# The start of a two-stage attention and feed-forward kernel: a row of maxima computed in two parts, one weight block converted two pairs later, and the second pair's maxima placed among the first pair's key tiles

## The chip, the cores and the metric

The kernel runs on one core of one Trainium2 chip. The metric is the device time of one execution in microseconds (us); a median of a few runs is given, and one further execution was profiled. Below, PE is the engine of matrix products, PEld its weight loads, DVE the vector engine, ACT the engine of activation functions, POOL the general engine, and SP the engine that only issues transfers here. Each runs its own instructions in order and waits for the others through semaphores.

## The reference

The first stage is an attention over 8 batches and 8 heads, with 1152 positions and a head size of 64. Queries are averaged over neighbouring positions, so that 576 remain. The second stage takes its 4608 rows of 512 numbers through a feed-forward block with the function h - tanh(h).

```python
q_pool = q.reshape(B, H, S // factor, factor, D).mean(axis=3)        # factor 2
scores = scale * np.matmul(q_pool, k.transpose(0, 1, 3, 2))
scores = scores - np.max(scores, axis=-1, keepdims=True)
attn = np.exp(scores)
attn = attn / (np.sum(attn, axis=-1, keepdims=True) + 1e-09)
attn_out = np.matmul(attn, v)
...
h = x @ w_in                                                         # 4608 x 512 by 512 x 2048
g = h - np.tanh(h)
return (g @ w_out).astype(np.float32)
```

## The kernel before

Two heads are worked on together as a *pair*: one lies in partitions 0 to 63, the other in 64 to 127. There are 32 pairs. The program numbers them from 0 (`pi`), so its `pi == 1` is "the second pair", or "pair 2", of the text.

For each pair the kernel does this:

- `load` (line 185) fetches the queries and keys, `load_v` (196) the values. `query_sums` (201) adds neighbouring queries: on DVE for the first pair, on POOL for the others.
- `hi_part` (209) makes a rounded copy of queries and keys on ACT, in three pieces; `lo_part` (213) makes what the rounding left out on DVE, in one piece of 1728 columns. Scores are products of these: hi by hi, hi by lo, lo by hi.
- `max_part` (217) computes a rough score tile for 128 queries by 384 keys, for both heads, from the hi parts alone, and DVE takes the largest of each row from PSUM. A pair needs fifteen: five tiles of queries (`t`) by three of keys (`c`).
- `max_rows` (229) takes the largest of the three key parts, negates it (tile `nm`), and turns it by a transpose (tile `tr`). Its inner `back` has SP write ten small transfers that lay the result out as one row per head (tile `mb`): for each `t` and each head one.
- `scores` (246) computes a tile of 128 keys by 288 queries (one half of the queries) for both heads: three products and a fourth, of ones with `mb`, which subtracts the maximum. ACT takes the exponential into a tile `p_f`.
- After the nine key tiles of a half, `pv` (269) multiplies the exponentials with the values. POOL adds the nine tiles up in three groups (`z_part`, 261), and after the second half PE sums those over the partitions (`z_sums`, 282).

Score tiles, rough score tiles, pv groups and two steps of a weight block all take their PSUM space from one pool of four buffers in turn (`banks`, 172). A tile can be written only when the one four places earlier has been read.

Beside this the attention stage converts the feed-forward weights, which arrive as 64-bit numbers, into a hi and a lo part. `w_block` (331) does one block of 128 by 512 weights over 75 units (below): it issues the load at unit `u`, has ACT and DVE begin at `u + 31` (one operation and three), DVE go on at `u + 49` (two), POOL add at `u + 50`, ACT split at `u + 66`, POOL subtract at `u + 68`, and SP store the result at `u + 75`. There are 32 blocks.

The order of all this is written out by hand. Time is cut into *units*: a pair has `U` = 36 of them, 18 to a half, and every second unit of a half has one score tile, with pv at the end of the half. `add(u, f, ...)` puts a step into a table for unit `u`; in each unit the tables run in the order `first`, `early`, the score tile, `at`, pv. The reduction of a rough score tile is put into `first` of the next unit. Units below 0 are what runs ahead of the first score tile. All engines keep this program order in the attention stage (`InOrder`, line 27), and SP's one queue of transfers too.

The steps of a pair are given as offsets from its first unit (lines 411 to 432). For the first pair the fifteen maxima stand at -60 to -46, the row at -43, its transfers at -42, the low part at -41, the values' load at -40. For the second pair, eight maxima stand at its offsets -54 to -38, which are units -18 to -2, and seven at units 0 to 16; its low part stands at unit 0, its row at 17, the transfers at 20. The third pair's loads stand at unit -14, its query sums at 1, its hi part at 17, and its first eight maxima at 18 to 34.

Weight blocks start at `36 * (i - 2) + 5`: block 1 at -31, block 2 at 5, block 3 at 41. Block 0 starts at 23.

The feed-forward stage then runs over chunks of 512 tokens, with sixteen slices of the hidden size in each; the change does not touch it.

In the profile nearly all operations of the attention stage carry line 37, that of the helper that records them. They are told apart by their tiles: `mx<-ps` is the reduction of a rough score tile, `p_f<-ps` the exponential, `ps<-p_f,v` pv, `mb<-tr` the row transfers, `w` and `w_raw` a weight block.

Of the kernel before, what the change touches and what calls it, by code (L numbers as in the profile page):

```python
# [12 lines left out]
ALU = mybir.AluOpType  # L13
AX = mybir.AxisListType
# [29 lines left out]
def kernel(  # L44
# [89 lines left out]
    t, n = chunks.pop()  # L134
# [4 lines left out]
    with ExitStack() as actx:  # L139

        sm = actx.enter_context(tc.tile_pool(name="sm", bufs=2))
        op = actx.enter_context(tc.tile_pool(name="op", bufs=1))
# [7 lines left out]
        pe, act, dve, pool, sp = (InOrder(tc, e) for e in (nc.tensor, nc.scalar, nc.vector, nc.gpsimd, nc.sync))  # L150
# [4 lines left out]
        U = 4 * KT  # L155
# [14 lines left out]
        at, first, early = {}, {}, {}  # L170
# [6 lines left out]
        def add(u, f, *args, at=at):  # L177
            at.setdefault(u, []).append(lambda: f(*args))
# [47 lines left out]
                pe.matmul(ps[:, h, 0:CH], w.hi[r, q0:q0 + P], w.hi[r, mv], start=True, stop=True)  # L226
            add(u + 1, lambda: dve.tensor_reduce(w.mx[:, :, t, c], ps[:, :, 0:CH], axis=AX.X, op=ALU.max), at=first)

        def max_rows(u, pi, step):

            w = pairs[pi]
            nm, tr = nms[w.i], sm.tile([P, 32], F32, name="tr")
            dve.tensor_reduce(nm[:, 0:10], w.mx.rearrange("p h t c -> p (h t) c"), axis=AX.X, op=ALU.max, negate=True)
            dve.transpose(tr, nm.bitcast(F32))

            def back():
                for t in range(5):
                    for h in range(2):
                        row, c = w.mb[64 * h:64 * h + 1].bitcast(F32), 5 * h + t
                        if t < 4:  # L240
                            sp.dma_start(row[:, t * P:(t + 1) * P].rearrange("p (g n) -> p g n", n=32), tr[c:P:32])
                        else:
                            sp.dma_start(row[:, t * P:].rearrange("p (g n) -> p g n", n=32), tr[P - (SQ - t * P) + c:P:32])
            add(u + step, back)
# [139 lines left out]
            for r in range(f // P, (f + WB) // P):  # L384
                blocks.append((1, r, 0))
        for i, blk in enumerate(blocks):
            u = U * (i - 2) + 5 if i else 23
            add(u, w_block, u, *blk)

        tot = []  # L390
# [20 lines left out]
        for pi in range(n_pair):  # L411
            u = pi * U
            units = dict(load=-86, query_sums=-71, hi=-55, lo=-36, load_v=-30)
            row, step = -19, 3

            spots = [x for half, us in ((-54, (2, 4, 8, 10, 12, 14, 16)), (-36, (2, 4, 8, 10, 14, 16)))
                     for x in [(early, half)] + [(at, half + i) for i in us]]
            if pi == 0:
                units.update(load=-70, query_sums=-62, hi=-60, lo=-41, load_v=-40)
                spots = [(at, -60 + i) for i in range(15)]  # L420
                row, step = -43, 1
            if pi == 1:
                units.update(load=-104, query_sums=-62)
            add(u + units["load"], load, pi)
            add(u + units["query_sums"], query_sums, pi, dve if pi < 1 else pool)
            for c in range(0, KQ, SQ):
                add(u + units["hi"], hi_part, pi, c, c + SQ)
            add(u + units["lo"], lo_part, pi)
            for i, (when, x) in enumerate(spots):
                add(u + x, max_part, u + x, pi, i // 3, i % 3, at=when)  # L430
            add(u + units["load_v"], load_v, pi)
            add(u + row, max_rows, u + row, pi, step)

        def run(u, at=at):

# [115 lines left out]
    for ci, (t0, n) in enumerate(chunks):  # L551
        x_h, x_l, _ = xs
        po = []
        for fc in range(NF):
# [3 lines left out]
            load = []  # L558
            if ci + 1 < len(chunks):
# [3 lines left out]
                load = [xs[2][(fc - x) // 3][i] for i, x in ((3, 3), (0, 0), (1, 2), (2, 2)) if (fc - x) % 3 == 0 and 0 <= fc - x < 3 * NP]  # L563
# [47 lines left out]
```

## Time and profile before

| what | value |
|---|---|
| median of 3 runs | 1610.8 us (1610.68 to 1611.51) |
| the profiled execution's own time | 1611.35 us |
| its span in the profile | 1609.6 us |
| PE busy | 1584.2 us, 98% |
| DVE busy | 1235.9 us, 77% |
| ACT busy | 1015.9 us, 63% |
| POOL busy | 1016.9 us, 63% |
| first pv group of the first pair starts | 44.49 us |
| second pv group of the first pair starts | 55.97 us |

A row of a timeline gives the start in us, the length in us, the engine, the line, the operation, the tile written and the tiles read, the shapes and how many instructions were merged; in brackets stands the idle time before it and what ended it. A row of a table of stretches gives start and end, the length, the busy time of PE, PEld, DVE, ACT and POOL with the number of instructions in brackets, the granted clock of PE as a share, the share of time in which the transfer engines were busy, and GB/s. Matmuls overlap: the step from one row's start to the next tells how fast they follow each other, the length of a row is longer.

### The profile page before, as it was taken

How to read it: one execution, taken by the hardware profiler on the slowest of the kernel's cores; microseconds unless marked ns; L12 is line 12 of the kernel's file. 1: busy time of each engine (PE TensorE's matmuls, PEld its weight loads, DVE VectorE, ACT ScalarE, POOL GpSimd, SP SyncE). 2: the span in 40 equal slices, each digit the busy share in tenths (PEclk: the TensorE clock that was granted, in tenths of full speed). 3: DMA queues.
4: the chain of work that ended last, by engine and by line, in shares of the span. 5: the costliest groups of instructions: out<-in, count | busy, mean ns of one | idle time of the engine just before them, and what ended most of it. 6: DMA issues, size and time to landing. Idle time of an engine off the chain costs nothing. (4 is left out here: it accounts for less than half of the span.)

```text
span 1609.6 us, 31923 instructions
## 1 busy us (share of the span) xinstructions
PE 1584.2 (98%) x12288; PEld 1233.6 (77%) x12288; DVE 1235.9 (77%) x1725; ACT 1015.9 (63%) x1833; POOL 1016.9 (63%) x760
## 2 busy tenths in 40 slices
PE   5999999999999999999999999999999999999999
PEld 3777777777777777777778888888888888888897
DVE  7888788787887888788567777767777777777786
ACT  1665665665665665666666666666665666666786
POOL 2899999999999999999845343334343343423332
PEclk9999999999999999999999999999999999999999
DMA  3343443443443443444474101111010111110100
GB/s 144 117 145 110 144 140 109 138 146 110 128 155 111 133 140 122 128 142 148 136 262 152 40 27 40 40 40 28 26 53 27 49 31 40 33 34 14 36 24 22
DMA packets 73433, 147.38 MB, mean 92 GB/s; under 512 B 12736, under 2 KB 37440, under 8 KB 73280
## 3 DMA queue, kind: packets, MB, share of 16 engines
q1 hardware_dynamic: 73280, 145.33, 27.4%
q8 instruction: 97, 1.59, 0.4%
q14 instruction: 56, 0.46, 0.1%
HBM read 109.20 MB, written 35.95 MB: 90 GB/s over the span
## 5 line engine op out<-in xcount | busy, mean ns | idle before, releaser
L37 DVE TENSOR_REDUCE mx<-ps 128x2 f32<-128x768 f32 x480 | 435.6, 953 | 111.3 <-PE ps L37 111.1
L37 POOL TENSOR_TENSOR g_lo<-g_s,g_hi 128x512 fp32r<-128x512 f32 (+1 forms) x160 | 190.8, 1192 | 482.7 <-ACT g_hi L514 445.0
L37 ACT ACTIVATE p_f<-ps 128x576 f32<-128x576 f32 x576 | 356.6, 651 | 78.9 <-PE ps L37 56.4
L37 PE MATMUL ps<-hi 64*128 64x288 f32 (+1 forms) x2112 | 316.3, 351 | 19.5 <-DVE mx L37 8.2
L37 PE MATMUL ps_h<-x,wi 128*128 128x512 f32 (+1 forms) x1440 | 318.3, 370 | 0.0
L37 PE MATMUL ps_o<-wo,g_hi 128*128 128x512 f32 x1008 | 311.5, 390 | 0.0
L37 POOL TENSOR_TENSOR z<-p_f 128x576 f32<-128x576 f32 x192 | 276.3, 1439 | 41.7 <-ACT p_f L37 39.9
L37 PE MATMUL ps<-p_f,v 128*64 128x288 f32 x2304 | 293.5, 409 | 0.0
L37 PEld LDWEIGHTS ps_h<-x,wi 128*128 128x128 f32 x1440 | 253.2, 188 | 50.4
L37 POOL TENSOR_TENSOR z<-z,p_f 128x576 f32<-128x576 f32 x192 | 273.3, 1423 | 15.0
L37 PEld LDWEIGHTS ps<-hi 64*128 64x128 f32 x2112 | 196.3, 187 | 91.0 <-issue 29.6
L37 PEld LDWEIGHTS ps<-p_f,v 128*64 128x64 f32 x2304 | 159.7, 137 | 113.9 <-ACT p_f L37 11.6
L503 ACT ACTIVATE g_u<-ps_h 128x512 f32<-128x512 f32 (+1 forms) x160 | 88.8, 555 | 235.7 <-PE ps_h L37 232.3
L508 DVE SCALAR_TENSOR_TENSOR ps_w<-g_u,ps_h 128x512 f32<-128x512 f32 (+1 forms) x160 | 103.0, 644 | 157.8 <-ACT g_t L504 157.2
L37 PEld LDWEIGHTS ps_o<-wo,g_hi 128*128 128x128 f32 x1008 | 187.6, 188 | 39.1
L37 PE MATMUL ps_o<-wo,g_lo 128*128 128x512 f32 x504 | 196.2, 389 | 0.0
L37 PE MATMUL ps<-hi,lo 64*128 64x288 f32 x1152 | 171.0, 293 | 0.0
L37 PE MATMUL ps<-lo,hi 64*128 64x288 f32 x1152 | 171.0, 293 | 0.0
L37 PE MATMUL ps<-mb,ones_k 64*128 64x288 f32 x1152 | 170.8, 293 | 0.0
L37 ACT ACTIVATE o_s<-ps 128x288 f32<-128x288 f32 x64 | 26.4, 412 | 218.5 <-PE ps L37 218.5
L513 DVE COPY_PREDICATED g_s<-g_m,g_t 128x512 f32<-128x512 int32 (+1 forms) x160 | 115.4, 721 | 16.8 <-DVE g_s L512 0.5
L511 DVE SCALAR_TENSOR_TENSOR ps_w<-g_s,ps_w 128x512 f32<-128x512 f32 (+1 forms) x160 | 102.9, 643 | 16.6 <-ACT g_m L507 0.5
(66 smaller groups left out, 2252.1 us busy)
## 6 DMA issues: line engine op xcount, KB each, us to landing
q_n<-in_q_dram SPq DMA_DIRECT2D x32, 576.0 KB
kq<-in_k_dram SPq DMA_DIRECT2D x32, 576.0 KB
v<-in_v_dram SPq DMA_DIRECT2D x32, 576.0 KB
x_dram<-o_s SPq DMA_DIRECT2D x32, 288.0 KB
out_dram<-o_s SPq DMA_DIRECT2D x34, 256.0 KB
w_raw<-in_moe_w_in_dram SPq DMA_DIRECT2D x16, 512.0 KB
wi_dram<-w_hl SPq DMA_DIRECT2D x16, 512.0 KB
w_raw<-in_moe_w_out_dram SPq DMA_DIRECT2D x16, 512.0 KB
```

Source lines behind the costliest of these rows:

```text
L37: ins = self.tc.keep_in_program_order(f(*args, **kwargs))
L503: nc.scalar.activation(u, h, AF.Square)
L508: nc.vector.scalar_tensor_tensor(w, u, -P0, h, op0=ALU.add, op1=ALU.mult)
L511: nc.vector.scalar_tensor_tensor(w, s2, P2, w, op0=ALU.add, op1=ALU.mult)
L513: last = nc.vector.copy_predicated(s1, m.bitcast(I32), th).ins
```

## The change

The first pair's row of maxima is made in two parts: `max_rows` takes a range of query tiles, and runs once for tiles 0 to 2 after nine maxima (unit -51) and once for tiles 3 and 4 after all fifteen (unit -43). Six transfers belong to the first part, four to the second. The load of the first pair's values moves from unit -40 to -50, just ahead of the first part's transfers.

Weight block 1 starts at unit 95 instead of -31; its first conversion then falls at unit 126, in the fourth pair.

For the second pair, the query sums move from unit -26 to -54 and the hi part from -19 to -46. All fifteen maxima stand at units 0 to 20 (twelve in the first half, three in the second), the low part at 18 instead of 0, the row at 21 and its transfers at 24. The first eight maxima of the third pair move from units 18 to 34 to units 22 to 34.

```diff
-        def max_rows(u, pi, step):
+        def max_rows(u, pi, step, t0=0, t1=5):
...
-            dve.tensor_reduce(nm[:, 0:10], w.mx.rearrange("p h t c -> p (h t) c"), axis=AX.X, op=ALU.max, negate=True)
+            dve.tensor_reduce(nm[:, 0:10].rearrange("p (h t) -> p h t", t=5)[:, :, t0:t1], w.mx[:, :, t0:t1], axis=AX.X,
+                              op=ALU.max, negate=True)
             dve.transpose(tr, nm.bitcast(F32))
 
             def back():
-                for t in range(5):
+                for t in range(t0, t1):
...
         for i, blk in enumerate(blocks):
-            u = U * (i - 2) + 5 if i else 23
+            u = U * (i - 2) + 5 if i > 1 else 23 + 2 * U * i
             add(u, w_block, u, *blk)
...
             if pi == 0:
-                units.update(load=-70, query_sums=-62, hi=-60, lo=-41, load_v=-40)
+                units.update(load=-70, query_sums=-62, hi=-60, lo=-42, load_v=-50)
                 spots = [(at, -60 + i) for i in range(15)]
                 row, step = -43, 1
+                add(u - 51, max_rows, u - 51, 0, 1, 0, 3)
             if pi == 1:
-                units.update(load=-104, query_sums=-62)
+                units.update(load=-104, query_sums=-90, hi=-82, lo=-18)
+                spots = [(early, -36)] + [(at, i - 36) for i in (1, 2, 4, 5, 7, 8, 10, 11, 13, 14, 16)] + [(early, -18), (at, -18), (at, -16)]
+                row = -15
+            if pi == 2:
+                spots[:8] = [(at, i - 72) for i in (22, 23, 25, 26, 28, 30, 32, 34)]
...
-            add(u + row, max_rows, u + row, pi, step)
+            add(u + row, max_rows, u + row, pi, step, 0 if pi else 3)
```

## The prediction

> **What bounds the kernel now.** I read the page's head, then stretches of ten microseconds (start and end, length, then busy time of PE, weight loads, DVE, ACT, POOL), then the waits of PE.
>
> ```profile
> span 1609.6 us, 31923 instructions
> PE 1584.2 (98%) x12288; PEld 1233.6 (77%) x12288; DVE 1235.9 (77%) x1725; ACT 1015.9 (63%) x1833; POOL 1016.9 (63%) x760
> ...
> 20.00:30.00 10.00, 5.51 (x20) 2.71 (x22) 9.80 (x12) 0.00 (x0) 0.00 (x0) 1.00 0.21 65
> 30.00:40.00 10.00, 5.17 (x38) 4.40 (x38) 6.56 (x7) 2.78 (x5) 5.83 (x3) 1.00 0.74 278
> ...
> PE ps L37 <- DVE mx L37: 8.2, 22, 2.6
> PE ps L37 <- ACT hi L37: 6.9, 1, 6.9
> PE ps L37 <- DVE w L37: 4.1, 1, 4.1
> PE ps L37 <- POOL z L37: 1.3, 1, 1.3
> ```
>
> PE is busy for 98% of the span, and its idle time of 25.4 us (1609.6 - 1584.2) lies almost wholly in the start: between 20 and 40 us PE is idle for 9.3 us. The waits name DVE's maxima and one wait of 4.1 us for a weight tile. A microsecond saved in the start should therefore come off the end, since from there on PE has next to nothing else to wait for. The timeline of the start shows why PE stops:
>
> ```profile
> 27.25 0.43 SPq L37 DMA_DIRECT2D w_raw<-in_moe_w_in_dram  x1
> 30.98 0.44 PE L37 MATMUL ps<-mb,ones_k 64*128 64x288 f32 x2
> 32.62 0.62 ACT L37 ACTIVATE ps<-w_raw 128x512 f32<-128x512 f32 x1 [21.69 <-DMA w_raw<-in_moe_w_in_dram]
> 33.18 1.17 ACT L37 ACTIVATE p_f<-ps 128x576 f32<-128x576 f32 x2
> 33.28 0.70 DVE L37 TENSOR_SCALAR ps<-ps 128x512 f32<-128x512 f32 x1 [3.33 <-ACT ps L37]
> 35.48 0.93 PE L37 MATMUL ps<-hi 64*128 64x384 f32 x4 [4.05 <-DVE w L37]
> ```
>
> PE has two score tiles ready at 31.4, but ACT, which runs in order, stands at the conversion of a weight block whose load was issued only at 27.25 and landed at 32.6. Both exponentials wait behind it; so does DVE, whose three operations on that block stand ahead of the next maxima. All four PSUM buffers are then held, and PE stops until 35.48. The load is late because SP, also in order, issues ten row transfers first:
>
> ```profile
> 7.58 13.06 DVE L37 TENSOR_REDUCE mx<-ps 128x2 f32<-128x768 f32 x15 [2.12 <-PE ps L37]
> 9.11 1.83 ACT L37 ACTIVATE hi<-kq 128x576 fp32r<-128x576 f32 x3 [1.73 <-POOL kq L37]
> 21.11 1.92 DVE L37 TENSOR_TENSOR lo<-kq,hi 128x1728 fp32r<-128x1728 f32 x1
> 21.28 5.49 SPq L37 DMA_DIRECT2D mb<-tr  x10
> 27.73 0.43 SPq L37 DMA_DIRECT2D q_n<-in_q_dram  x1
> ```
>
> DVE sets the pace of the start: fifteen maxima in 13.06 us (0.87 each), the row, the low part, and then eight maxima of the second pair ahead of the first score.
>
> **The change, part by part.** I count up to the start of the second probabilities-times-values group (pv) of the first pair, at 55.97. By there the changed order has put through the same maxima: fifteen of pair 1, fifteen of pair 2, eight of pair 3. I call a maximum "m" and a score tile "S"; these rows price them, with PE's slow cadence and its fast one:
>
> ```profile
> 38.23 0.61 PE L37 MATMUL ps<-hi 64*128 64x288 f32 x2 [0.78 <-DVE mx L37]
> ...
> 39.35 0.44 PE L37 MATMUL ps<-hi 64*128 64x288 f32 x2
> ...
> 40.31 0.76 PE L37 MATMUL ps<-hi 64*128 64x384 f32 x4
> 40.56 0.65 ACT L37 ACTIVATE p_f<-ps 128x576 f32<-128x576 f32 x1 [0.31 <-PE ps L37]
> 40.87 0.44 PE L37 MATMUL ps<-lo,hi 64*128 64x288 f32 x2
> ...
> 42.16 0.96 DVE L37 TENSOR_REDUCE mx<-ps 128x2 f32<-128x768 f32 x1 [0.32 <-PE ps L37]
> ...
> 43.11 0.30 PE L37 MATMUL ps<-lo,hi 64*128 64x288 f32 x2
> ...
> 44.49 4.59 PE L37 MATMUL ps<-p_f,v 128*64 128x288 f32 x36
> ...
> 49.82 0.29 PE L37 MATMUL ps<-hi 64*128 64x288 f32 x2
> 50.35 0.55 PE L37 MATMUL ps<-hi 64*128 64x384 f32 x4
> 50.74 0.30 PE L37 MATMUL ps<-lo,hi 64*128 64x288 f32 x2
> ...
> 52.85 4.42 DVE L37 TENSOR_REDUCE mx<-ps 128x2 f32<-128x768 f32 x5 [0.30 <-PE ps L37]
> ...
> 55.97 4.59 PE L37 MATMUL ps<-p_f,v 128*64 128x288 f32 x36
> ```
>
> Slow: S is 40.31 - 39.35 = 0.96, of four matmul pairs at 0.24; the next pairs (m, and the first of an S) take 0.56, so m is 0.32. Fast: S 0.53 (50.35 - 49.82), a matmul pair a quarter of it, 0.13, m 0.39 - 0.13 = 0.26. On DVE m is 0.88 back to back (4.42 / 5). A pv group is 4.5 at the fast cadence. The cadence rose at 43.1, 4.9 us after the last gap.
>
> *Row in two parts.* It adds a reduction, a transpose and no transfer (six and four for ten). From the end of the maxima at 20.64 to the low part at 21.11 the existing two cost 0.47 on DVE; this is paid once more, after nine maxima. The low part then runs 21.58 to 23.5. It is on the path: +0.47. The first six row transfers can go at about 16.0 (7.58 + 9 x 0.87 + 0.6) and at 0.55 each (5.49 / 10) are issued by 19.3, four microseconds before a score needs them; with one queue they were issued by 24.6. The other four go by 23.8 and are wanted only in the second half, after 38. The load of values now passes the rows on SP: one issue slot of some 0.4 us, long before 16.0.
>
> *Weight block moved.* ACT's 0.62 and DVE's five operations leave the first pair, and the wait for the load with them; nothing then stands ahead of the first exponential. SP reaches the third pair's loads near 24 rather than at 27.73.
>
> *Maxima of pair 2 behind the scores.* Query sums and high part move up in their queues without new work: ACT had run the high part by 10.9 us already, right after POOL's sums. DVE has no maxima between the low part and the first score. Now the first half, by hand: the first S can go on at 23.6. PE at 0.96 and 0.32 is continuous while slow, and DVE takes each m as it comes: the fourth leaves PE at 23.6 + 0.72 + 3 x 0.32 + 2 x 0.96 = 27.2 (the first was issued earlier) and is reduced by 28.35, with 0.2 from PE to the reader (ACT's row at 40.56 begins 0.25 after its tile's slot) and 0.96. After some 5 us the cadence rises, and DVE at 0.88 sets the pace through four buffers: the twelfth m can be issued when the tenth is reduced, at 28.35 + 6 x 0.88 = 33.6. Pv follows at about 34.05. Bounds: DVE without a gap, 23.5 + 10 x 0.88 + 0.5 = 32.8; PE slow throughout, 23.6 + 0.72 + 8 x 0.96 + 11 x 0.32 = 35.5. I take 34.05, for the rise at 43.1 came after one gapless stretch of the kind that follows here. It was 44.49.
>
> Pv takes 4.5 to 38.55, and the low part of pair 2, now due there, hides under it: 1.9 of 4.5, after DVE's last maxima at 35.4; without that cover it would cost the 1.9 in full. Second half: eleven m where there were eight, plus the row of pair 2. DVE starts at 39.05 (38.55, an m and the 0.2), and must finish nine maxima and the row before the last m gets its buffer: 9 x 0.88 + 0.45 = 8.4, to 47.4; with the m itself pv starts at 47.9. PE alone would need 9 x 0.53 + 11 x 0.26 = 7.6, so DVE bounds this half, which lasts 2.3 longer than before (9.3 + 4.5 against 55.97 - 44.49 = 11.5). Gain so far 55.97 - 47.9 = **8.1**; with the bounds of the first half 6.7 to 9.3.
>
> The new order puts the fourth pair's loads ahead of pair 2's rows on SP. The key load needs the buffer that the low part frees at 37.4, and the rows' transposed input is ready only near 42.3, so they still wait for DVE, not SP: issued by 47.9, wanted at about 54.
>
> *Where the block goes.* These stretches are whole pairs; the first two are pairs 2 and 3, which carry an extra block today:
>
> ```profile
> 62.22:86.41 24.19, 24.19 (x272) 17.74 (x274) 21.98 (x28) 15.63 (x27) 22.45 (x17) 1.00 0.40 131
> 86.41:111.05 24.64, 24.27 (x272) 17.76 (x274) 20.63 (x24) 15.63 (x28) 24.17 (x17) 1.00 0.48 150
> 111.05:135.28 24.23, 24.23 (x272) 17.80 (x274) 19.62 (x24) 15.08 (x27) 23.16 (x16) 1.00 0.40 130
> ...
> 208.41:232.65 24.24, 24.24 (x272) 17.79 (x274) 19.31 (x23) 15.10 (x26) 22.44 (x16) 1.00 0.40 131
> ...
> 88.31 0.40 PE L37 MATMUL ps<-hi 64*128 64x288 f32 x2 [0.37 <-DVE mx L37]
> ```
>
> The extra block cost 24.19 + 24.64 - 2 x 24.24 = 0.35, of which 0.37 is one wait for a maximum. The moved block lies exactly two pairs later, with the same neighbours, so pairs 4 and 5 pay **0.35** (bounds 0 and 0.8, twice that wait). DVE's 2.7 or so of added work there, and POOL's, is covered by PE at 24.2 a pair.
>
> Sum: 8.1 - 0.35 = 7.75, with bounds 5.9 to 9.3. The profiled execution took 1611.35 (span 1609.6), so it would take 1603.6 (span 1601.9); its median stands 0.55 lower at 1610.8, giving **1603.1**.
>
> **The rivals.**
>
> *PE's cadence falls back.* In the DVE-paced stretches PE works 0.53 + 4/3 x 0.26 = 0.88 of each 1.17 us. In the first maxima (15 in 13.06 us, each 0.32 of slow work in 0.87) it never rose; a gapless stretch raised it. What 75% does no row shows. If it falls, a pv begins slow: 4.9 us at 0.24 instead of 0.125 is 20 matmuls and 2.35 us lost, once or twice: 1605.5 to 1607.8, say 1606.6. The Trainium skill, "TensorE: Matmul & The Clock Gate", section "A second HAM failure mode: psum-queue depth-cycling", speaks for this: it tells of a kernel whose short idle times between groups, as it cycled through PSUM, made the clock swing between half and full rate. By that rule this case would come out near 1606.6; the trace of before has no warm stretch with such gaps to test it.
>
> *Slower: the cadence stays low for the whole first pair.* First half to 35.5, pv 36 x 0.24 = 8.6 to 44.1, eleven m and nine S at the slow price 12.2 to 56.3, pv to 64.9 against 60.5: 4.4 more, and 0.35: 1615.6. It decides once slow work adds over 7.75. Against it: each pv is gapless for longer than the 4.9 us that sufficed.
>
> *Nothing is gained: maxima don't run back to back.* In the row at 42.16 DVE idles 0.32 ahead of a 0.96 reduction. If all 23 in the first pair went so, 23 x (1.28 - 0.88) would cost 9.2 less the 1.5 of gaps that I counted at the first four: 7.7, and 1610.8. Against it stand the five in 4.42 at PE's fast cadence.
>
> *POOL is late.* It must do pair 3's query sums, when that load has landed, ahead of the sums z:
>
> ```profile
> 34.09 1.40 POOL L37 TENSOR_TENSOR kq<-q_n 128x576 f32<-128x576 f32 x1 [25.02 <-DVE ps L37]
> 35.44 3.12 POOL L37 TENSOR_TENSOR z<-p_f 128x576 f32<-128x576 f32 x1
> 38.64 1.41 POOL L37 TENSOR_TENSOR z<-z,p_f 128x576 f32<-128x576 f32 x1
> ```
>
> From issue to start were 6.4 us; from 24 that gives 30.4, query sums to 31.8, then six sums of pairs and triples (12 x 1.42 = 17.1, one lengthened by 1.7 beside a low part) to 50.6 at the earliest, and PE wants them at 52.4. Were POOL no earlier than now, it would end at 54.3: 1.9 lost, 1605.0.
>
> **How the numbers follow.** Forecast 0.68, its own range 1601.5 to 1604.9 by the bounds; cadence falls back 0.12; POOL 0.06; nothing gained 0.07; slower 0.07. No change is within 0.2%, 3.2 us, about what can be told here; so faster 0.86, same 0.07, slower 0.07. The range takes in the forecast's bounds and the two middle rivals, 1600.8 to 1608.2, and leaves out the last two.
>
> **What would show it.** Right: row transfers in two groups, near 16 and 21.6; the first exponential at 24 to 25 with no weight conversion ahead; pv at 33 to 35.5 and at 46.6 to 49; DVE without gaps in between; one wait of PE of about 0.4 around pair 5. Wrong: matmul pairs 0.24 apart after 31, a wait of PE for z near 52, or the first pv early and the second not.

## The result and the profile after

The changed kernel takes 1603.09 us (median of 6 runs, 1602.76 to 1603.29) against 1611.37 us of the kernel before, run beside it (median of 6, 1610.68 to 1612.22). The ratio is 0.9949, with a 95% interval of 0.9939 to 0.9959: faster by 0.5%, or 8.3 us. The profiled execution took 1603.26 us with a span of 1601.4, 8.2 less than the span before.

The head of the page and PE's waits (engine, tile, line, what it waited for; us in all, times, longest) of the changed kernel:

```profile
span 1601.4 us, 31921 instructions
PE 1580.5 (99%) x12288; PEld 1231.5 (77%) x12288; DVE 1236.8 (77%) x1727; ACT 1015.9 (63%) x1833; POOL 1014.0 (63%) x760
...
PE ps L37 <- ACT hi L37: 6.8, 1, 6.8
PE ps L37 <- DVE mx L37: 4.5, 17, 0.7
PE ps L37 <- DVE lo L37: 3.4, 1, 3.4
```

The wait of 4.1 for a weight tile is gone, that for maxima fell from 8.2 to 4.5, and a wait of 3.4 for the first pair's low part has come in: PE is now ready before DVE is. The waits are only about half of what came off, as the stretches up to the start of the second pv show (kernel before, then changed kernel):

```profile
0.00:55.97 55.97, 37.51 (x256) 25.11 (x256) 41.02 (x53) 18.37 (x30) 21.11 (x26) 1.00 0.34 122
0.00:47.92 47.92, 33.91 (x257) 23.03 (x257) 38.73 (x50) 18.34 (x29) 21.01 (x26) 1.00 0.39 146
```

PE is idle 4.45 us less (18.46 to 14.01) and busy 3.60 less, with the same products. Seven maxima fewer stand alone in PE's rows, where each counts 0.69 with its end instead of 0.32 in a row of products, and some three score tiles more run at the fast cadence; by these prices that is about 2.6 and 1.3, an estimate. Rows of the timeline of the start, changed kernel:

```profile
16.08 7.62 SPq L37 DMA_DIRECT2D mb<-tr  x10
21.52 1.92 DVE L37 TENSOR_TENSOR lo<-kq,hi 128x1728 fp32r<-128x1728 f32 x1
23.35 0.95 DVE L37 TENSOR_REDUCE mx<-ps 128x2 f32<-128x768 f32 x1
23.49 0.61 PE L37 MATMUL ps<-lo,hi 64*128 64x288 f32 x2 [3.41 <-DVE lo L37]
23.74 0.40 SPq L37 DMA_DIRECT2D q_n<-in_q_dram  x1
24.65 0.65 ACT L37 ACTIVATE p_f<-ps 128x576 f32<-128x576 f32 x1 [13.46 <-PE ps L37]
27.50 7.88 DVE L37 TENSOR_REDUCE mx<-ps 128x2 f32<-128x768 f32 x9 [0.32 <-PE ps L37]
27.83 1.43 POOL L37 TENSOR_TENSOR kq<-q_n 128x576 f32<-128x576 f32 x1 [18.50 <-DMA q_n<-in_q_dram]
28.30 0.30 PE L37 MATMUL ps<-mb,ones_k 64*128 64x288 f32 x2
34.08 4.59 PE L37 MATMUL ps<-p_f,v 128*64 128x288 f32 x36
35.29 2.89 DVE L37 TENSOR_TENSOR lo<-kq,hi 128x1728 fp32r<-128x1728 f32 x1
47.92 4.59 PE L37 MATMUL ps<-p_f,v 128*64 128x288 f32 x36
```

The first exponential starts at 24.65, where it stood at 33.18, with no weight conversion ahead of it. The two pv groups of the first pair start at 34.08 and 47.92 (44.49 and 55.97 before). So 8.05 us, nearly the whole difference, are there by the end of the first pair. The rest of the attention goes nearly as before, pair by pair. The stretches of pairs 4 to 6 follow, and the one wait of PE in pair 5:

```profile
103.02:127.27 24.25, 24.25 (x272) 17.79 (x274) 22.27 (x29) 15.64 (x27) 23.12 (x17) 1.00 0.39 130
127.27:152.01 24.74, 24.33 (x272) 17.75 (x274) 21.62 (x26) 15.51 (x27) 24.27 (x17) 1.00 0.48 151
152.01:176.26 24.25, 24.25 (x272) 17.78 (x274) 19.48 (x24) 15.08 (x27) 22.95 (x16) 1.00 0.38 130
...
129.14 0.40 PE L37 MATMUL ps<-hi 64*128 64x288 f32 x2 [0.34 <-DVE mx L37]
```

### The profile page after: what moved, and what is told of

It reads as the page before. It is cut to its first block, busy times and chain, and to the rows that moved or that the text cites. A ratio compares the mean times of both kernels' runs of the same rounds, so it can differ in the third digit from the quotient of the medians.

```text
span 1601.4 us, 31921 instructions
## 1 busy us (share of the span) xinstructions
PE 1580.5 (99%) x12288; PEld 1231.5 (77%) x12288; DVE 1236.8 (77%) x1727; ACT 1015.9 (63%) x1833; POOL 1014.0 (63%) x760
## 4 chain that ended last, share of the span: by engine, by line
PE 90%; DVE 1%; POOL 0%; ACT 0%; issue 0%; ACTq 0%; POOLq 0%
PE ps L37 41%; PE ps_h L37 25%; PE ps_o L37 25%; POOL z L37 0%; DVE lo L37 0%; DVE mx L37 0%; DVE w L37 0%; DVE ps L37 0%; ACT p_f L37 0%; ACT w_hl L37 0%; ACT x L553 0%; ACT ps L37 0%; ACT z_s L37 0%; ACTq L510 0%; ACTq L37 0%
## 5 line engine op out<-in xcount | busy, mean ns | idle before, releaser
L37 PE MATMUL ps<-hi 64*128 64x288 f32 (+1 forms) x2112 | 312.7, 349 | 11.6 <-ACT hi L37 6.8
```

The source lines that it names most:

```text
L37: ins = self.tc.keep_in_program_order(f(*args, **kwargs))
```

## The experiments: which part gave the gain

Three parts make up the change: the block (B), the row in two parts (R) and pair 2's maxima among the first pair's key tiles (M). The prediction gives DVE's order and one late load as the cause; by that the parts should not add. The rival is that each has its own worth. The kernel before ran beside every group of kernels, at medians of 1611.2 to 1611.5 us.

**The block alone.** The kernel before, with:

```diff
-            u = U * (i - 2) + 5 if i else 23
+            u = U * (i - 2) + 5 if i > 1 else 23 + 2 * U * i
```

> The kernel before with one part of the change alone: weight block 1 two pairs later (unit 95). My theory: the exponentials then wait for nothing and DVE loses three operations ahead of the low part of pair 2, which may start at 29.95 when the eight maxima end. By hand with the same prices (score tile 0.96 slow, maximum 0.32 on PE and 0.88 on DVE, low part 1.95), PE waits once, to about 33.0, for the first maximum after the low part, is gapless from there, and the first pv starts near 40.0 instead of 44.49, the second near 51.5 instead of 55.97. With 0.15 for the two pairs that carry the block: about 1607.1 us, 4.3 below before. Rival (only the wait for the load counts, DVE's share does not): 33.18 - 30.3 = 2.9 less, 1608.6. Rival (it gives all of the change's gain): 1603.

Measured: 1604.56 us (1604.08 to 1605.99), ratio 0.996 (0.9946 to 0.9973); its profiled execution took 1605.44, 5.9 less than that of the kernel before. That is more than the 4.3 expected and short of all. PE in its timeline:

```profile
28.16 0.61 PE L37 MATMUL ps<-hi 64*128 64x288 f32 x2 [0.18 <-DVE mx L37]
...
32.63 0.93 PE L37 MATMUL ps<-hi 64*128 64x384 f32 x4 [0.90 <-DVE mx L37]
...
36.71 0.29 PE L37 MATMUL ps<-lo,hi 64*128 64x288 f32 x2
...
38.69 4.59 PE L37 MATMUL ps<-p_f,v 128*64 128x288 f32 x36
```

Two things differ from the working by hand. The first score tile starts at 28.16, not at 29.14 as in the timeline of the kernel before:

```profile
28.27 0.69 PE L37 MATMUL ps<-hi 64*128 64x384 f32 x2 [1.04 <-DVE mx L37]
29.14 0.61 PE L37 MATMUL ps<-hi 64*128 64x288 f32 x2 [0.18 <-DVE mx L37]
```

There PE waited 1.04 for a maximum just ahead of the tile: the block's own steps take turns in the four PSUM buffers, and without them a buffer comes a maximum earlier. I had counted the block on ACT and DVE only. And the fast cadence was there 4.1 us after the last gap (32.63 to 36.71), not 4.9. Pv stands at 38.69 instead of the 40.0 expected, and the second, at 50.16, is 5.8 earlier than before.

**The block put back** into the changed kernel (the same line, the other way round):

> The changed kernel with weight block 1 back at unit -31, its other parts kept. My theory: the parts don't add. SP issues the block's load at 23.7, right after the row transfers, it lands near 27.8 (the queries issued at 23.74 in the changed kernel were there at 27.83); ACT's conversion and DVE's three operations hold the first exponential to 28.5 and DVE's first maximum of pair 2 to 30.5 instead of 23.35. PE stands until about 31.6, so the first pv comes near 40 instead of 34.08, the second 6 to 6.5 later than 47.92: about 1609.4 us, nearly all of the gain gone. Rival (the parts add, block worth 4.3 here as before): 1607.4. Rival (the block is hidden since its load is issued 3.5 us earlier): below 1605.

Measured: 1609.53 us (1609.29 to 1610.81), as my theory had it: R and M without B are worth 1.9. ACT, DVE and PE:

```profile
28.01 0.62 ACT L37 ACTIVATE ps<-w_raw 128x512 f32<-128x512 f32 x1 [17.06 <-DMA w_raw<-in_moe_w_in_dram]
28.66 0.70 DVE L37 TENSOR_SCALAR ps<-ps 128x512 f32<-128x512 f32 x1 [5.22 <-ACT ps L37]
30.87 0.61 PE L37 MATMUL ps<-hi 64*128 64x288 f32 x2 [5.97 <-DVE w L37]
```

The same wait is back, 6.0 us long: everything of the first pair now stands behind the block, on DVE too, which in the kernel before had eight maxima to do meanwhile.

**The row in one piece**, in the changed kernel:

```diff
-                add(u - 51, max_rows, u - 51, 0, 1, 0, 3)
...
-            add(u + row, max_rows, u + row, pi, step, 0 if pi else 3)
+            add(u + row, max_rows, u + row, pi, step)
```

> The changed kernel with the first pair's row of maxima in one piece after all fifteen, the other parts kept. My theory: DVE saves 0.4, but the first six row transfers are issued only between 21.3 and 24.6 and land about 1 us later, so the first score tile's fourth product starts near 25.9 instead of 24.14 and everything up to the second pv shifts by about 1.75: 1604.8 us. Rival (a score tile waits for all ten transfers, issued by 26.8): that product near 27.9, 1606.9. Rival (the transfers were in time anyway and only DVE's 0.4 counts): 1602.7.

Measured: 1604.97 us (1604.83 to 1605.37), 1.9 more than with the row in two parts. Rows of SP, PE and ACT tell why:

```profile
21.25 5.49 SPq L37 DMA_DIRECT2D mb<-tr  x10
25.17 1.26 PE L37 MATMUL ps<-mb,ones_k 64*128 64x288 f32 x2 [1.27 <-DMA mb<-tr]
26.47 0.65 ACT L37 ACTIVATE p_f<-ps 128x576 f32<-128x576 f32 x1 [15.55 <-PE ps L37]
```

The fourth product of the first score tile waits for the row, its two matmuls end at 26.43, and the exponential starts at 26.47, 1.8 later than in the changed kernel. The last of the ten transfers is issued only by 26.74, so the tile did not wait for all ten. By medians, B and M without R (1604.97) are not better than B alone (1604.56).

**The row in two parts alone**, in the kernel before (`max_rows` as in the diff of the change, and the line that calls it at unit -51):

> The kernel before with one part of the change alone: the first pair's row in two parts (its other steps where they were). My theory: SP is done with the row transfers near 23.8 instead of 26.77, so the values' and the weight block's loads go 3.0 us earlier; the block lands near 29.6 instead of 32.6, and the exponentials, DVE's three operations, and all that follows shift by 3.0: first pv near 41.5, 1608.4 us. Rival (the load is not what holds ACT): DVE's 0.4 only, 1611.8.

Measured: 1608.47 us (1607.6 to 1609.21). The block's load now goes at 24.14 instead of 27.25 and ACT has it 3.3 us earlier:

```profile
24.14 0.43 SPq L37 DMA_DIRECT2D w_raw<-in_moe_w_in_dram  x1
29.36 0.63 ACT L37 ACTIVATE ps<-w_raw 128x512 f32<-128x512 f32 x1 [18.33 <-DMA w_raw<-in_moe_w_in_dram]
```

Its first pv starts at 40.87, 3.6 before that of the kernel before. So the kernel before was held by a load queued behind ten small transfers.

**Block and row, without the maxima** (both edits in the kernel before):

> The kernel before with two parts of the change, the block two pairs later and the first pair's row in two parts; the maxima of pair 2 stay where they were. My theory: with the block gone nothing waits for SP's queue in the start, so the earlier row transfers are worth nothing as long as eight more maxima stand ahead of the first score, and DVE pays 0.4 more: 1605.0 us, against 1604.6 with the block alone. The move of the maxima is then worth 1.9 of the whole 8.3, and only together with the two-part row. Rival (the parts' gains of 6.9 and 2.9 add, and the move of the maxima is a loss of 1.5): 1601.6.

Measured: 1605.76 us (1604.59 to 1608.67). Its pv groups start at 39.05 and 50.52, each 0.36 after those of the block alone:

```profile
39.05 4.59 PE L37 MATMUL ps<-p_f,v 128*64 128x288 f32 x36
```

That is DVE's 0.4 for the second reduction and transpose; the earlier transfers bring nothing here. Together:

| parts | median us | less than before |
|---|---|---|
| B | 1604.56 | 6.9 |
| R | 1608.47 | 2.9 |
| B, R | 1605.76 | 5.5 |
| B, M | 1604.97 | 6.4 |
| R, M | 1609.53 | 1.9 |
| B, R, M | 1603.09 | 8.3 |

The parts don't add. R and B cure the same wait, so R on top of B is a small loss (0.36 by the profile, the runs scatter by more); M loses with B alone or R alone (0.4 and 1.1, the first within the spread of the runs) and gains 2.7 with both. M alone was not run. The values' load stands at unit -50 in the kernels with M and at -40 in B, in R and in B, R; its share was not measured apart.

## The experiments: what sets the pace now

**DVE's maxima made short.** In the changed kernel:

```diff
-dve.tensor_reduce(w.mx[:, :, t, c], ps[:, :, 0:CH], ...)
+dve.tensor_reduce(w.mx[:, :, t, c], ps[:, :, 0:P if pi == 1 else CH], ...)
```

> The changed kernel with DVE's maxima of pair 2 taken over 128 of the 384 keys of each tile; PE computes the tiles as before. This leaves out two thirds of that pair's maxima, so its rows of maxima are lower bounds. My theory (DVE sets the pace of the first pair's two halves): the first pv near 32.9 instead of 34.08, as PE's slow cadence up to 28.3 is the bound left; the second half goes at PE's 7.6 instead of 9.3, second pv near 45.1 instead of 47.92; 1600.3 us. Rival (PE and the buffers' hand-overs set the pace, DVE only follows): no change, 1603.1.

Measured: 1600.81 us (1600.63 to 1601.67), pv at 32.37 and 45.37:

```profile
32.37 4.59 PE L37 MATMUL ps<-p_f,v 128*64 128x288 f32 x36
45.37 4.59 PE L37 MATMUL ps<-p_f,v 128*64 128x288 f32 x36
```

DVE does set the pace: with less to do there, PE comes 2.5 us earlier to the second pv, though it computes the same tiles. That the second pv came close to the expected 45.1 is partly chance: the first came 0.5 early, and the second half took 8.5 instead of 7.6, as pair 3's eight maxima, left whole, still ran back to back on DVE there (6.99 us).

**Does the cadence fall when PE has gaps?** The prediction's first rival could not be judged from the trace of before. In the changed kernel it stays fast in the stretches that DVE paces, at PE's 75%. Two kernels make DVE slower, by taking pair 2's maxima twice, all of them or every second one:

```diff
-            add(u + 1, lambda: dve.tensor_reduce(w.mx[:, :, t, c], ...), at=first)
+            for _ in range(2 if pi == 1 else 1):          # the other kernel: "pi == 1 and (3 * t + c) % 2"
+                add(u + 1, lambda: dve.tensor_reduce(w.mx[:, :, t, c], ...), at=first)
```

> The changed kernel with each of pair 2's fifteen maxima taken twice by DVE. It is to show whether PE's cadence falls back when PE has more idle time: PE then works some 0.88 of 2.35 us in the first pair's first half, against 0.88 of 1.17. DVE's added work is 12 x 0.88 in the first half and 3 x 0.88 in the second, so the second pv comes some 12.5 later, near 60.4, and the time near 1615.6 us if the cadence stays. If it falls back, matmul pairs of a score tile follow at 0.24 instead of 0.13 in the first half, and the first pv takes up to 6.9 instead of 4.5: up to 2.4 more for each pv, 1618 to 1620. The prediction's rival took this for what might happen already at 75%.

> The changed kernel with every second of pair 2's fifteen maxima taken twice by DVE, so that PE at the fast cadence works 2.63 of 5.28 us, 50%, in the first pair's first half: between the 75% at which the cadence stayed and the 37% at which it fell. If it stays, matmul pairs of a score tile follow at 0.13 from about 29 on, pv takes 4.5, and the time is 1603.1 + 7 x 0.88 = 1609.3 us less up to 1; if it falls, pairs at 0.24 are seen again after 30 and a pv may take up to 6.9.

Measured, one run each: 1617.32 us with all twice, 1609.45 with every second one. PE with all twice, and two stretches of it (the granted clock is the third number from the end):

```profile
29.53 0.33 PE L37 MATMUL ps<-hi,lo 64*128 64x288 f32 x2
29.66 0.33 PE L37 MATMUL ps<-mb,ones_k 64*128 64x288 f32 x2
...
31.66 0.47 PE L37 MATMUL ps<-hi,lo 64*128 64x288 f32 x2
31.90 0.47 PE L37 MATMUL ps<-mb,ones_k 64*128 64x288 f32 x2
...
42.11 5.69 PE L37 MATMUL ps<-p_f,v 128*64 128x288 f32 x36 [0.21 <-DVE mx L37]
47.73 0.57 PE L37 MATMUL ps<-hi 64*128 64x384 f32 x4
...
61.80 4.59 PE L37 MATMUL ps<-p_f,v 128*64 128x288 f32 x36
...
24.00:28.00 4.00, 3.79 (x30) 3.15 (x28) 3.93 (x5) 1.95 (x3) 0.13 (x1) 1.00 0.78 260
32.00:42.00 10.00, 7.97 (x48) 5.49 (x45) 9.83 (x12) 2.98 (x5) 4.35 (x4) 0.50 0.12 49
```

Steps between pairs are 0.13 at 29.5 and 0.24 at 31.7: the cadence had risen and fell again, and the granted clock from 32 to 42 is 0.50. It fell once more near 54.6 (0.50 from 56 to 60). The first pv took 5.6 (42.11 to 47.73) instead of 4.5. The second started at 61.80, 1.4 later than the 60.4 expected of DVE's work. With every second one, PE:

```profile
35.42 0.33 PE L37 MATMUL ps<-hi,lo 64*128 64x288 f32 x2
35.56 0.33 PE L37 MATMUL ps<-mb,ones_k 64*128 64x288 f32 x2
...
38.18 4.59 PE L37 MATMUL ps<-p_f,v 128*64 128x288 f32 x36
42.70 0.57 PE L37 MATMUL ps<-hi 64*128 64x384 f32 x4
```

Steps stay near 0.13 and pv at 4.5, though single gaps of PE last 1 us. So here the rival is a real mechanism. By one run of each, it sets in between 50% and 37% of work, and the change stays clear of it. Whether the share counts or how often and how long PE stops (gaps up to 0.98 in the one, up to 1.26 and closer together in the other) these two runs do not separate. The Trainium skill, "TensorE: Matmul & The Clock Gate", section "A second HAM failure mode: psum-queue depth-cycling", describes such a fall; the 37% run agrees, the 50% and 75% runs show that short gaps alone don't bring it.

## The experiments: a faster version

PE's new wait of 3.4 is for a low part on DVE, while POOL is idle. In the changed kernel:

```diff
-            dve.tensor_tensor(w.lo, w.kq, w.hi.bitcast(F32), op=ALU.subtract)
+            (dve if pi else pool).tensor_tensor(w.lo, w.kq, w.hi.bitcast(F32), op=ALU.subtract)
```

> The changed kernel with the first pair's low part computed by POOL instead of DVE; POOL has nothing to do between 9.3 and 27.8 us there. By POOL's 1.4 us for 576 columns it takes some 4.2 us and is done near 13.6. My theory: DVE's order sets the end of the first pair, so its 1.9 come off, and PE's wait of 3.4 for the low part goes: DVE's first maximum of pair 2 at 21.5 instead of 23.35, and less idle time of DVE at the first four maxima (1.3 in all), since PE is ahead by then. First pv between 30.8 and 32.3 instead of 34.08, time 1600.0 to 1601.3, say 1600.5 us. Rival (another thing bounds the first scores, the row transfers or PE's slow cadence): 1602.5 to 1603.1.

Measured: **1599.74 us** (1599.7 to 1600.13), ratio to before 0.9928 (0.9915 to 0.994), 3.35 less than the changed kernel. POOL, DVE and PE:

```profile
9.59 3.86 POOL L37 TENSOR_TENSOR lo<-kq,hi 128x1728 fp32r<-128x1728 f32 x1
21.48 10.54 DVE L37 TENSOR_REDUCE mx<-ps 128x2 f32<-128x768 f32 x12
30.71 4.59 PE L37 MATMUL ps<-p_f,v 128*64 128x288 f32 x36
44.53 4.59 PE L37 MATMUL ps<-p_f,v 128*64 128x288 f32 x36
```

DVE takes pair 2's twelve maxima without a gap from 21.48 on: the 1.9 of the low part came off, and the gaps of DVE at the first maxima too. Both pv groups are 3.4 earlier. The time and the first pv lie just below the ranges expected, which had left DVE some idle time at the first maxima.

Two more steps were tried on top. Six and nine instead of eight and seven of pair 3's maxima:

```diff
+                spots = [(at, i - 72) for i in (22, 24, 26, 28, 30, 32)] + [(early, -36)] + [(at, i - 36) for i in (2, 4, 6, 8, 10, 12, 14, 16)]
```

> The changed kernel with the first pair's low part on POOL, and two of pair 3's first eight maxima moved out of pair 1's second half into pair 2's first half (six and nine instead of eight and seven). My theory: DVE sets the pace of pair 1's second half, which falls from 9.3 to about 7.3 us, near PE's own 9 x 0.53 + 9 x 0.26 = 7.1; pair 2's first half grows by PE's 0.52 and, with DVE's 9 x 0.88 = 7.9 there against PE's 7.1, by 0.3 to 0.8 more: 1598.5 to 1599.0 us against 1599.7 with the low part alone. Rival (pair 2, which carries two weight blocks, has no room on DVE, and the two maxima come back as waits of PE there): 1599.7 or above.

and with that weight block 0 in pairs 6 and 7 (`23 + 2 * U * (2 - i)`):

> As the one with two maxima moved, and weight block 0 taken out of pair 2 as well (unit 167 instead of 23, so that it falls into pairs 6 and 7). My theory: DVE then has 2.7 us more room in pairs 2 and 3 and the wait of 0.36 near 80 goes, while pairs 6 and 7 pay what pairs 4 and 5 pay for block 1 (0.13 net): about 1598.2 us. Rival (the moved maxima have room anyway): the same as without the move of block 0, within 0.3.

Measured: 1599.48 us (1599.18 to 1600.28) and 1600.81 us (1599.61 to 1602.44). Neither is a gain that these runs can tell from the low part on POOL alone. With the two maxima moved, pair 1's second pv comes at 43.63, 0.9 earlier and not 2.0 (its first pv stood 0.3 later in this run, so the half itself is 1.2 shorter), and the way to pair 2's first pv grows by 0.75 (first row; second row: without the move):

```profile
43.63:57.15 13.52, 13.52 (x152) 9.60 (x150) 12.56 (x13) 7.17 (x13) 12.64 (x9) 1.00 0.31 107
```

```profile
44.53:57.30 12.77, 12.77 (x148) 9.08 (x146) 10.68 (x12) 6.74 (x13) 10.93 (x7) 1.00 0.33 111
```

PE has no idle time left in either stretch: the two maxima cost there what PE needs for them, 2 x 0.26, and some 0.2 more. Moving block 0 as well brought none of the further gain expected.

## Why the prediction was right, point by point

- *What bounds the kernel.* Right: 8.05 of 8.2 us of the span come from before 48 us, and nothing later took them back. But the prediction's opening speaks of idle time alone, and that fell by 4.45; the rest is the same products following one another more closely and more of them at the fast cadence, which its sum took in through the slow and fast prices.
- *Row in two parts.* Transfers expected near 16.0 and done by 23.8, the low part 21.58 to 23.5; measured 16.08 to 23.70, with the second group from 21.62, and from 21.52, the next maximum at 23.35. The cost of 0.47 came out as 0.41 (the low part at 21.52 instead of 21.11).
- *Weight block.* Its removal freed ACT, DVE and SP as told. Its share of the PSUM buffers, 1 us in the kernel before, was not among the terms; it didn't reach the sum, since I built the new start from its own steps and did not subtract waits from the old one.
- *First half.* DVE's fourth maximum expected done by 28.35: the row at 27.50 begins with it, so by 28.46. Pv 34.05, measured 34.08.
- *Second half.* Pv 47.9, measured 47.92. The low part under the first pv took 2.89, not 1.9, and still hid: DVE waited 0.9 for PE after it.
- *Where the block goes.* The term was too large. The wait came, at 129.14, 0.34 long. But I set the pairs against 24.24, while pairs 5 and 6 took 24.50 and 24.38 before. Pairs 4 to 6 now take 73.24 us against 73.11 then (111.05 to 184.16 before): 0.13 and not 0.35.
- *Rivals.* The cadence rose at 28.3, 4.8 after the last gap, and stayed. That 4.8 is so near the 4.9 of the trace of before is chance: in the kernel with every second maximum twice, whose PE rows go the same way up to there, the rise came after some 3.3. POOL was earlier than I feared: the third pair's load was there at 27.83, not 30.4. The 6.4 us that I took from issue to start became 4.1 (23.74 to 27.83); before, two other loads had been issued just ahead of it. PE's wait for z after the first pair did not appear. Maxima ran back to back (nine in 7.88).

The forecast gain was 7.75 and the measured one 8.2 by spans, 8.3 by medians. That the predicted median hit 1603.1 owes something to the starting value: the 1610.8 shown was 0.6 below the median of six. Of the 0.45 missing, 0.22 is the block's term; the rest lies in single pairs later on and was not traced; the runs of one kernel scatter by more.

## What to carry to other kernels

In a start where several in-order engines wait for one late load, write the new order out instruction by instruction with the prices of the trace, and look which engine has no gap: that one's list is the time. Subtracting the waits that an edit removes would have missed here: PE's idle time fell by 4.5 and the time by 8.2, two parts cure the same wait, and the third loses with either of them alone. Then ask what else on that list an idle engine could do; moving one operation to POOL gave 3.35 us more.

## What was not expected of the hardware

PE's cadence (0.24 against 0.13 per pair) fell at 37% of work and held at 50%, with single gaps of 1 us. The granted clock in the profile's rows does not always tell which cadence it is: it stood at 1.00 at the slow cadence of the start (24 to 28 us above) and at 0.50 where the cadence had fallen again (32 to 42). The cadence was up 4.1, 4.8 and 4.9 us after the last gap in the three kernels shown and some 3.3 after it in the one with every second maximum twice, which fits the window of about 3.4 us that runs on its own, told by the Trainium skill, "TensorE: Matmul & The Clock Gate", "Part 1: The HAM clock gate". A low part of 1728 columns took DVE 1.92 alone, but 2.89 beside POOL's sums in the changed kernel, where a sum had begun 0.3 before it. In the kernel before it began 0.1 ahead of such a sum: there it took 1.96, and the sum 3.12 instead of 1.41. In both cases the one that began second was lengthened; no run tests why.
